# Memory attention and a bilinear feed-forward layer: batch 1's k and v apart, zero products ahead, and a new order of the work

## The chip, the core and the metric

The kernel runs on one core of a Trainium2 chip. The core has a matrix engine (PE, with its weight loads shown apart as PEld), a vector engine (DVE), an engine for activations (ACT), GpSimd (POOL), and SyncE (SP), which here only starts output transfers. All read the on-chip memory SBUF; PE writes to eight accumulator banks called PSUM, from which DVE and ACT read. Transfers from and to HBM are issued by an engine into a queue and run on 16 DMA engines.

The metric is the device time of one execution in microseconds, the median of several runs. Each engine executes its own instructions strictly in the order written; an instruction waits on semaphores for what it needs from other engines or transfers, and what stands behind it on its engine waits too.

## The reference

For each of 8 batches and 8 heads (576 tokens, 64 dimensions a head) the tokens' k and v are pooled into 32 memory slots, then attention runs over the slots, and the joined heads go through a bilinear layer:

```python
a = softmax(phi)                                # over the 32 slots, per token
k_m, v_m = einsum('bhsm,bhsd->bhmd', a, k), ... # the same with v
attn = softmax(q @ k_m.T / 8) @ v_m             # over the slots
x = attn, heads joined: 4608 x 512
out = ((x @ w_a) * (x @ w_b)) @ w_out           # 512 -> 1536 -> 512
```

## The kernel before

**Tiling and stages.** For a batch, `exp_phi` (ACT) makes the exponentials of phi, `exp_sb`. Products of `exp_sb` with k, v and a plane of ones then give, for all heads, the k sums, the v sums and the sums of the exponentials at once (`kv_sums`, tile `pkv`; 72 small products of 64 rows by 32 columns of the array). `take_kv` scales them by the reciprocal of the third part, `kv_transpose` turns them (`pT`, `kvT`). q is turned on DVE (`qT`), `scores` multiplies it with the turned k part (`pscore`), ACT takes the exponential (`E`), and E is normalised over the slots (`A`). The v part is never multiplied with A directly: `fold` multiplies it with the weights `w_a` and `w_b` first (`pva`, cast into `vab0` and `vab1`), so that A times `vab` is at once the input of the bilinear layer. The rows L727 are these products (`pa`, `pb`); ACT casts `pa`, and DVE multiplies it with `pb` into `ht`. From batch 5 on part of the products is made by a scheme of seven instead of eight products (L750). The output product with `w_out` goes the same way (L654), on sums of `ht` (`h_sums`, L638) and of the weights (`w_sums`, L621), two blocks of 128 tokens at a time.

Batch 0 has its own path: `sums` (tile `pk`, L377) and `transpose` (L395), separately for k and v and for two groups of heads. Batch 1 has its q in two parts (320 and 256 tokens), and its scores, exponentials and normalisation are made per part (`scores_half`, L442).

**The order.** `PLAN` (from L18) is a list written out by hand or by a program: each word is one step, and the loop at L785 issues the steps in this order. So the place of a word sets the order on every engine at once. Words used below: `0ks1` is sums of batch 0, group 1, with k (`vs` with v), `0kt1` its turn; `1kv`, `1km0`, `1kvt` are `kv_sums`, `take_kv` and `kv_transpose` of batch 1; `0qt0` a turn of q; `1qh30` a turn of a part of q; `0s0`, `1sh0` scores, `0e0` their exponential, `den` the sums over slots, `nr` the normalisation; `0hv0a` and `1v2b` are folds with w_a or w_b, `hx`, `x` their casts; `a0.1.0`, `b0.1.0` are `pa` and `pb` of batch 0, 128 columns number 1, first part of the tokens; `d3` is three steps of the output product; `h`, `g` are `h_sums` on POOL or DVE; `T`, `V` are `w_sums` on POOL or DVE; `p1`, `k1`, `v1`, `q1.0`, `wa0:256`, `o1` are the loads of phi, k, v, a part of q, of columns 0 to 255 of w_a, of a part of w_out; `F1` is a zero product, `O` makes the block `ones` for the sums over slots, `M` fills the plane of ones of the second k/v buffer.

**Loads.** All input but batch 0's k is loaded by transfers that POOL issues, in one queue, so in order. POOL waits before such an issue until the one eight loads earlier has landed. k and v of even and odd batches lie in two buffers `kv_sb0` and `kv_sb1`, each with its own plane of ones (filled by DVE at L236 and by POOL at L792).

**Zero products.** `fill` (L227) multiplies a zero block `warm` with itself into the PSUM bank that would be taken next, without taking it: 128 by 128 times 128 by 512, result unused. The list before has nine of them, one at the start and eight between 15.9 and 22.6 us. Two calls that follow each other make two tiles on the same bank, and the second waits for the first.

Of the kernel before, what the change touches and what calls it, by code (L numbers as in the profile page):

```python
# [8 lines left out]
F32 = mybir.dt.float32  # L9
F16 = mybir.dt.float16  # L10
# [3 lines left out]
P = 128  # L14
# [9 lines left out]
1qh10 1qh00 o0 o3 1sh0 1eh00 0v1b 1v1b 1x0b1 1eh10 1x0a1 0x1b0 1den00 0x1b1 1x1b1 o4 1den10 o2 a0.6.1 b0.6.0 b0.6.1
b0.5.1 1nr10 1nr00 1x1b0 b0.4.0 a0.7.1 b0.7.1 a0.7.0 a0.5.0 b0.7.0 a1.5.0 b0.5.0 h0.3 b1.5.0 a1.3.0 1qh21 a0.4.1 o5
b1.3.0 1qh31 1qh01 a1.4.0 b0.4.1 a1.1.0 1qh11 a1.2.0 b1.4.0 a1.0.0 b1.1.0 1sh1 0v2a 1eh01 1eh11 0x2a1 b1.0.0 0x2a0
b1.2.0 1den01 a1.6.0 0v2b 0x2b0 0x2b1 b1.6.0 v2 a0.9.1 1v2b 1v2a 1x2b0 1x2b1 a0.11.1 1x2a1 1x2a0 b0.9.1 a0.10.1
a0.9.0 b0.11.1 b0.10.1 b0.9.0 V20 1den11 a1.10.0 b1.10.0 a0.11.0 b0.11.0 a0.8.0 a1.11.0 b0.8.0 b1.11.0 1nr11 d1
1nr01 a0.10.0 d1 V00 a1.8.0 b0.10.0 a1.7.0 d1 b1.8.0 p2 V21 a1.11.1 b1.7.0 b1.11.1 d1 a1.3.1 a1.0.1 a1.2.1 g0.0 d1
b1.3.1 a1.6.1 d1 b1.2.1 b1.0.1 V01 a0.8.1 V10 a1.4.1 a1.9.0 d1 k2 2exp0 2exp1 g0.1 d1 V11 b1.6.1 V31 a1.5.1 p3 g0.2  # L30
b0.8.1 q2 d1 b1.4.1 d3 a1.1.1 b1.9.0 d6 2kv 3exp0 k3 d2 2km0 d1 a1.9.1 2km1 v3 d3 b1.5.1 d1 3exp1 d1 a1.10.1 d2
a1.8.1 2kvt b1.1.1 d2 h1.0 a1.7.1 2qt1 d4 2qt0 2qt3 2v1b 2x1b1 2v0a 2x1b0 T30 2qt2 2x0a1 d12 2x0a0 d4 g2.0 g1.1 2sc
g1.2 2e0 b1.7.1 d1 2e1 g1.3 q3 d2 b1.8.1 d3 b1.10.1 d1 2den0 d1 g2.1 p5 2den1 d1 b1.9.1 d1 2nr0 d5 2v2b 3kv 2v1a
g2.3 2x2b1 3km0 2nr1 2x2b0 2x1a1 d7 3km1 d6 3qt2 2x1a0 2v0b 2v2a 2x0b1 3qt3 d3 3qt0 2x2a1 d3 a2.6.0 d1 b2.6.0 d1
3qt1 a2.4.0 2x2a0 b2.4.0 d1 h2.2 d1 a2.7.0 d2 a2.4.1 d1 2x0b0 b2.4.1 d4 a2.3.0 a2.1.1 3kvt 5exp1 v5 b2.7.0 p4 b2.3.0
a2.8.0 b2.1.1 k5 a2.1.0 d2 a2.2.0 d2 q4 d1 a2.5.0 h3.3 3sc 3e0 d2 b2.2.0 d1 3e1 d2 b2.8.0 5exp0 d1 b2.1.0 v4 d2
a2.10.0 d2 b2.10.0 a2.0.1 a2.11.0 b2.11.0 b2.5.0 3den0 a2.0.0 d1 b2.0.1 h3.0 d1 g3.1 a2.5.1 d1 a2.9.0 k4 b2.5.1 h3.2
b2.0.0 3nr0 a2.11.1 d1 a2.8.1 b2.9.0 d1 3den1 d2 a2.10.1 d2 b2.10.1 d1 3v0a 3nr1 3x0a1 5kv 3x0a0 3v0b 3x0b0 b2.8.1
a2.2.1 d1 q5 d1 4qt0 b2.11.1 4qt3 4exp1 d1 3x0b1 d3 b2.2.1 d1 a2.9.1 d1 4qt1 d2 4qt2 d1 a2.7.1 b2.9.1 g4.3 d1 a2.6.1
h4.0 a2.3.1 d1 g4.1 d1 a3.3.0 d1 h4.2 4exp0 k7 b2.7.1 a3.2.0 d2 b2.6.1 d5 b3.3.0 b3.2.0 d2 4kv p6 3v2a 4km0 d2 3x2a1  # L40
4km1 d11 3x2a0 b2.3.1 d2 4kvt d2 a3.0.0 a3.3.1 v6 5km0 q6 d2 a3.1.0 5km1 k6 h5.0 d5 b3.1.0 a3.1.1 4sc 4e0 b3.0.0 d1
5qt3 d2 b3.1.1 5qt0 d1 a3.0.1 4e1 d3 b3.3.1 d5 3v1b 3v1a 4ed 3v2b 3x1b1 d5 3x1a0 d2 3x1a1 4sm0 d1 5qt1 d2 h5.3 3x2b0
5kvt a3.8.0 4sm1 d1 3x1b0 h5.1 3x2b1 d4 5qt2 d3 a3.6.1 b3.0.1 a3.10.0 d3 a3.4.0 d1 p7 d1 6exp1 d1 b3.8.0 b3.4.0 d1
a3.5.0 b3.6.1 d1 b3.10.0 4tn1 a3.7.0 a3.9.0 h5.2 d1 5sc 4tn0 5e0 d1 b3.5.0 5e1 a3.5.1 a3.11.0 d1 b3.7.0 d3 6qt0 d4
4v0a 4x0a0 4v1b 4v0b 4x0b1 d2 4x1b1 d5 6qt2 d1 4ad d1 5ed d1 a3.4.1 5sm0 b3.5.1 d2 b3.9.0 d1 4x1b0 d3 4x0a1 b3.11.0
d2 q7 d3 6qt1 d1 a3.6.0 a3.2.1 h6.3 6exp0 b3.6.0 d2 b3.4.1 d2 4x0b0 a3.8.1 a3.7.1 d5 a3.11.1 d2 b3.11.1 b3.8.1 d1
5tn0 d2 b3.2.1 4v2b 4v2a 4x2b0 6kv h6.0 4v1a d2 4x2b1 d1 5sm1 4x2a0 6km1 6km0 h6.1 6qt3 d3 b3.7.1 4x1a1 d3 4x1a0
a3.9.1 d2 4x2a1 5tn1 d2 b3.9.1 d3 a3.10.1 a4.0.0 g6.2 a4.2.1 b3.10.1 b4.0.0 d1 a4.3.0 d2 a4.0.1 6kvt b4.2.1 a4.6.0
d5 5ad 5v1a 6sc 5x1a1 h7.3 d1 6e1 d1 5x1a0 d1 7qt0 b4.6.0 d1 6e0 b4.0.1 d6 5T0D d2 h7.0 5v1b 5v0a 5v0b 5x1b0 g7.1
g8.0 g8.3 5x1b1 5T1D g7.2 5x0a0 d3 5x0b0 d6 5x0a1 b4.3.0 d8 5S01D a4.9.1 5T3D v7 a4.7.0 g8.1 b4.7.0 a4.10.1 a4.8.0  # L50
d1 b4.9.1 d1 5x0b1 a4.1.1 d2 5S11D 5S31P b4.8.0 b4.10.1 6ed 5S21P a4.6.1 a4.11.0 d1 b4.6.1 a4.5.0 d1 P5.4.1 7exp0
b4.5.0 b4.11.0 d1 b4.1.1 d3 P5.5.1 P5.4.2 a4.2.0 P5.5.2 d3 5S00P a4.1.0 d1 7qt3 5T2P P5.4.6 a4.9.0 h8.2 d1 a4.4.0
6sm0 d1 P5.5.5 b4.2.0 d1 7exp1 d1 6tn0 d1 b4.9.0 P5.4.5 P5.4.7 d1 P5.5.6 d3 P5.5.3 d1 a4.8.1 d2 b4.1.0 d1 5S10P d1
P5.4.3 P5.4.4 a4.4.1 a4.7.1 5S20P b4.4.1 d2 b4.4.0 d1 b4.8.1 5v2a 7qt2 5v2b 5x2a0 P5.5.7 5x2b0 b4.7.1 d4 5x2a1 6sm1
a4.10.0 a4.3.1 b4.3.1 d2 5x2b1 P5.5.4 P5.1.1 a4.11.1 b4.10.0 h9.3 d1 6tn1 d6 5S30D a4.5.1 d1 P5.2.1 P5.1.6 d1 J5.5
g9.0 a5.10.1 d1 P5.1.5 P5.2.2 d1 b4.11.1 d1 H5.4 h9.1 P5.1.7 d3 P5.1.2 d1 P5.2.5 d2 P5.2.6 d2 P5.1.3 P5.6.1 d1
P5.1.4 d1 P5.2.3 a5.11.0 d1 P5.2.7 d2 P5.7.1 a5.8.0 h9.2 d1 b4.5.1 P5.7.5 P5.6.6 P5.2.4 d3 P5.7.6 d1 P5.6.5 d1
P5.6.2 H5.1 P5.7.3 H5.2 d5 h10.0 P5.7.2 P5.6.7 a5.8.1 P5.3.1 P5.7.7 P5.6.3 b5.11.0 P5.0.1 d3 h10.1 d2 P5.6.4 P5.0.5
P5.3.6 P5.7.4 d1 b5.10.1 P5.0.6 d3 a5.9.0 6ad H5.7 d2 H5.6 P5.0.3 P5.3.2 d1 P5.3.5 d3 P5.0.2 d1 P5.3.7 d2 P5.0.7 d1
h10.3 a5.10.0 d1 P5.3.3 d3 6T0P d1 P5.3.4 d1 P5.0.4 d1 6T1P 6v0a 6x0a0 6x0a1 6T2P 7qt1 7kv 6v2b 6v0b H5.0 7km0 d1  # L60
H5.3 d1 6x2b1 d1 7km1 d4 6x0b0 6x0b1 d1 b5.8.0 6x2b0 d2 6T3P a5.11.1 b5.10.0 7kvt d1 b5.9.0 d3 6S00P d2 6v1a 7sc
6S10D d3 6x1a0 d1 7e1 d1 g11.0 6S30D g10.2 7e0 b5.8.1 6x1a1 d1 b5.11.1 d6 6v2a 7v1a 6v1b 6x2a1 g11.1 d1 6x1b0 6S20D
# [21 lines left out]
def kernel(  # L84
# [196 lines left out]
    def units(b):  # L281
# [269 lines left out]
        def one(f, *a):  # L551
            return lambda: f(*a)
# [289 lines left out]
```

## Time and profile before

| | us |
|---|---|
| median of 3 runs | 235.27 (233.99 to 237.27) |
| span of the profiled execution | 232.1 |
| PE busy | 214.1 (92%) |
| weight loads busy | 163.6 (70%) |
| DVE busy | 195.7 (84%) |
| ACT busy | 169.4 (73%) |
| POOL busy, with its issues of transfers | 138.2 (60%) |

Busy time counts an instruction from its start to its end; PE's products overlap each other, so a busy PE may still not stream at its best. The profile's page also cuts the span into 40 slices and gives the busy share of each in tenths:

```profile
PE   1189879999999998999999999999999999999993
DVE  3543899999987667898988999999999999999942
ACT  2206679987899997589978996977897769785330
POOL 7927233812549597893374099499475991881151
```

A slice is 5.8 us long. PE reads 1 in the first two, where it has little to do, and 9 in nearly all from the seventh on; DVE reads 9 from the seventh to the eleventh; POOL issues the loads in the first two.

### The profile page before, as it was taken

To read this page: it belongs to the slowest core of one execution; us is meant where nothing else is said; L and a number is where in the kernel's file an instruction comes from. 1 tells how busy PE (TensorE), PEld (TensorE's weight loads), DVE (VectorE), ACT (ScalarE), POOL (GpSimd) and SP (SyncE) were. 2 spreads that over 40 slices of the span, in tenths; PEclk is the share of its full clock that TensorE was granted. 3 is DMA by queue.
4 is the path that set the end of the run, shared out by engine and by line. 5 is a ranking of instruction groups with operands and counts; after the bars stand their busy time and mean duration, and the time that the engine had idled before them with its cause. 6 is when DMAs were issued, how large, how long until landed. Compare 5 with 4: busy or idle time off the path is not lost.

```text
span 232.1 us, 7493 instructions
## 1 busy us (share of the span) xinstructions
PE 214.1 (92%) x2906; PEld 163.6 (70%) x2906; DVE 195.7 (84%) x517; ACT 169.4 (73%) x450; POOL 138.2 (60%) x139
## 2 busy tenths in 40 slices
PE   1189879999999998999999999999999999999993
PEld 0143537588778777777777787887778877888882
DVE  3543899999987667898988999999999999999942
ACT  2206679987899997589978996977897769785330
POOL 7927233812549597893374099499475991881151
PEclk9999999999999999999999999999999999999999
DMA  6999999999998999999840902121303303032164
GB/s 229 238 199 256 205 205 205 205 259 258 208 284 138 264 207 243 253 241 254 210 93 4 190 1 65 28 64 32 93 3 90 78 16 92 18 77 55 42 158 111
DMA packets 26259, 34.09 MB, mean 147 GB/s; under 512 B 2000, under 2 KB 20304, under 8 KB 26224
## 3 DMA queue, kind: packets, MB, share of 16 engines
q0 software_dynamic: 19760, 23.14, 53.5%
q1 hardware_dynamic: 5952, 9.70, 16.2%
q10 hardware_dynamic: 512, 0.79, 1.0%
q8 instruction: 22, 0.36, 0.6%
q14 instruction: 13, 0.11, 0.1%
HBM read 42.47 MB, written 9.44 MB: 224 GB/s over the span
## 4 chain that ended last, share of the span: by engine, by line
PE 71%; DMA 17%; POOL 6%; ACT 3%; issue 2%; DVE 1%; POOLq 0%
PE py L654 18%; PE pb L727 11%; PE pa L727 11%; PE pv L654 9%; DMA wb_sb<-in_moe_w_b_dram 6%; DMA kv_sb<-in_k_dram 6%; PE py L750 5%; PE px L654 4%; PE pva L516 4%; DMA kv_sb<-in_v_dram 4%; PE pv L750 3%; POOL h_sums L638 2%; PE pkv L323 2%; PE px L750 1%; ACT vab L548 1%
## 5 line engine op out<-in xcount | busy, mean ns | idle before, releaser
L734 DVE TENSOR_TENSOR ht<-a_sb,pb 128x288 f16<-128x288 f16 (+2 forms) x144 | 60.5, 445 | 9.6 <-PE pb L727 5.3
L727 PEld LDWEIGHTS <-vab 128*128 128x128 f16 x576 | 55.3, 98 | 14.9 <-issue 2.4
L731 ACT CAST a_sb<-pa 128x288 f16<-128x288 f32 (+2 forms) x144 | 55.1, 417 | 13.6 <-PE pa L727 8.9
L727 PE MATMUL pb<-A,vab 128*128 128x288 f16 (+2 forms) x288 | 54.9, 286 | 0.1
L727 PE MATMUL pa<-A,vab 128*128 128x288 f16 (+2 forms) x288 | 54.3, 286 | 0.5 <-DVE A L478 0.4
L548 ACT CAST vab<-pva 128x512 f16<-128x512 f32 x82 | 45.4, 611 | 6.9 <-PE pva L516 6.8
L654 PEld LDWEIGHTS <-h_sums 128*128 128x128 f16 x432 | 41.4, 98 | 9.9 <-issue 2.4
L638 POOL TENSOR_TENSOR h_sums<-ht 128x768 f16<-128x768 f16 x19 | 31.2, 1645 | 21.4 <-DVE ht L734 21.3
L654 PE MATMUL py<-w_sums,h_sums 128*128 128x256 f16 x216 | 38.1, 273 | 0.0
L654 PEld LDWEIGHTS <-ht 128*128 128x128 f16 x324 | 31.2, 98 | 7.5 <-issue 2.2
L654 PE MATMUL pv<-wo_sb,h_sums 128*128 128x256 f16 x216 | 36.4, 273 | 0.0
L638 POOL TENSOR_TENSOR h_sums<-ht,h_sums 128x768 f16<-128x768 f16 x10 | 16.4, 1640 | 11.6 <-DVE h_sums L638 11.5
L755 ACT COPY z<-py 128x288 f32<-128x288 f32 x48 | 19.2, 415 | 2.3 <-PE py L750 1.8
L781 POOL TENSOR_TENSOR ht<-ah,bh 128x288 f16<-128x288 f16 x19 | 13.7, 737 | 10.1 <-DVE ah L759 7.1
L654 PE MATMUL px<-wo_sb,ht 128*128 128x256 f16 x108 | 18.9, 273 | 0.0
L654 PE MATMUL py<-wo_sb,ht 128*128 128x256 f16 x108 | 18.8, 273 | 0.0
L654 PE MATMUL py<-w_sums,ht 128*128 128x256 f16 x108 | 18.4, 273 | 0.0
L661 ACT ACTIVATE u<-py 128x256 f32<-128x256 f32 x36 | 14.4, 399 | 4.0 <-PE py L654 3.9
L425 ACT ACTIVATE E<-pscore 128x288 f16<-128x288 f32 x28 | 9.8, 431 | 9.5 <-PE pscore L412 9.4
L291 ACT ACTIVATE exp_sb<-phi_sb 128x576 f16<-128x576 f32 x16 | 10.9, 692 | 5.2 <-DMA phi_sb<-in_phi_dram 5.2
L300 DVE STREAM_TRANSPOSE qT<-q_sb 128x288 f32<-128x288 f32 x28 | 12.2, 456 | 2.6 <-DMA q_sb<-in_q_dram 2.6
L750 PE MATMUL py<-asum,vab 128*128 128x288 f16 x48 | 13.5, 286 | 0.0
(106 smaller groups left out, 383.0 us busy)
## 6 DMA issues: line engine op xcount, KB each, us to landing
out_dram<-o_sb SPq DMA_DIRECT2D x68, 128.0 KB, 2.4
phi_sb<-in_phi_dram POOLq DMA_DIRECT2D x8, 576.0 KB, 10.3
kv_sb<-in_v_dram POOLq DMA_DIRECT2D x8, 576.0 KB, 11.2
kv_sb<-in_k_dram POOLq DMA_DIRECT2D x7, 576.0 KB, 13.5
q_sb<-in_q_dram POOLq DMA_DIRECT2D x6, 576.0 KB, 11.9
wo_sb<-in_moe_w_out_dram POOLq DMA_DIRECT2D x6, 256.0 KB, 14.0
wa_sb<-in_moe_w_a_dram POOLq DMA_DIRECT2D x2, 512.0 KB, 14.2
wb_sb<-in_moe_w_b_dram POOLq DMA_DIRECT2D x2, 512.0 KB, 16.6
```

Source lines behind the costliest of these rows:

```text
L291: nc.scalar.activation(out=t["exp"][:, 2 * z:2 * z + 2, :, :], in_=phis[b][:, 2 * z:2 * z + 2, :].rearrange("p c (i m) -> p c i m", m=M), ...
L300: nc.vector.transpose(out=t["qT"][:, hp, :].bitcast(F32), in_=qs[b][:, hp, :].bitcast(F32))
L548: engine_copy(out=vabs[b][z][:, g, lo:hi], in_=pva[:, 0:hi - lo])
L638: engine.tensor_tensor(out=out, in0=in0, in1=in1, op=op)
L654: nc.tensor.matmul(po, lhs[:, i], rhs[:, i], start=first and i == 0, stop=i == KH - 1, skip_group_check=not first)
L661: nc.scalar.mul(out=x, in_=po, mul=scale)
L727: nc.tensor.matmul(ps, vabs[b][x][:, g, P * i:P * (i + 1)], attn[b][:, g, ts], start=(g == 0), stop=(g == 1))
L731: nc.scalar.copy(out=a_sbs[b, i, hf][:, :n], in_=ps)
L734: nc.vector.tensor_tensor(out=ht[:, i, t0:t0 + n], in0=a_sbs.pop((b, i, hf))[:, :n], in1=ps, op=ALU.mult)
L750: nc.tensor.matmul(x[bank][0], lhs, rhs, start=first, stop=True, skip_group_check=True)
L755: nc.scalar.copy(out=x[name], in_=po)
L781: engine.tensor_tensor(out=ht[:, i, t0 + HALF:t0 + S], in0=x["ah"], in1=x["bh"], op=ALU.mult)
```

## The change

The list is new as a whole. Beside it:

- Batch 1's k and v are summed apart: `1kp` sums k with the ones (128 columns), `1vp` sums v alone (64 columns), `1kg`, `1vg` scale them, `1kx`, `1vx` turn them. So the scores of batch 1 can be made ahead of its v. Batches 2 to 7 keep `kv_sums`.
- Both k/v buffers lie in one tile `kv_all` of five planes: k, v of even batches, the ones, k, v of odd batches. One block of ones serves both, so `M` is gone. For odd batches the ones come first in the sums.
- The three blocks `vsum` come from a pool that rotates three buffers instead of two fixed ones.
- 46 zero products instead of nine: 30 ahead of batch 0's first sum, eight from there to the first `pa`, eight behind that.
- The loads go: phi, q, v of batch 0, then `q1.1`, `wa0:256`, `wb0:256`, `wa256:512`, `p1`, `k1`, `q1.0`, `v1`, `wb256:512`, and the other weights. Before, v of batch 0 was followed by the first half weights, `p1`, `k1`, `v1`, then `wa512:1024`, `q1.0`, `wb512:1024`, `wa1024:1536`, `q1.1`, `wb1024:1536`. `O` stands at the front, ahead of `q1.1`.
- Ten operations on sums (of `h`, `w`, `v`, `A`, and products of `ah`, `bh`) go from DVE to POOL.
- `slot_sums` and its branch in `kv_sums`, which the list did not use, are taken out.

```diff
 PLAN = """
-wb0:256 0qt0 wa0:256 0qt3 wb256:512 0qt1 wa256:512 p1 0exp0 0exp1 F1 0ks0 0kt0 0ks1 0vs1 0vt1 0vs0 0vt0 M k1 F1
-0hv0a 0s0 v1 0qt2 O 0kt1 0e0 F1 0s1 0e1 0hx0a0 0hx0a1 F2 0den10 0den01 0den11 0den00 wa512:1024 0hv0b 0hx0b0 0hx0b1
...
+F1 F1 F1 F1 F1 F1 F1 F1 F1 F1 0qt0 F1 F1 F1 O F1 F1 F1 F1 F1 F1 F1 F1 0exp0 q1.1 F1 F1 F1 F1 F1 0qt1 F1 0qt3 0qt2 F1
+0exp1 F1 wa0:256 F1 0ks1 F1 0ks0 F1 0kt1 0s1 F1 F1 0kt0 0e1 0den11 0vs1 0s0 wb0:256 0e0 F1 0vs0 F1 F1 wa256:512 0den10
+0vt1 0vt0 0den01 0nr11 0hv0a 0nr01 1qh01 F1 0hv0b 0hx0a1 0hx0a0 a0.1.1 p1 0den00 F1 k1 q1.0 0hx0b1 v1 1qh11 0hx0b0 F1
+0nr00 0nr10 0hv1a 0hx1a0 a0.0.1 b0.0.1 wb256:512 1exp1 F1 a0.0.0 wb512:1024 1qh21 a0.1.0 b0.1.0 0hx1a1 1exp0 1kp 1kg0
+a0.2.1 F1 1kg1 a0.3.1 wa512:1024 wa1024:1536 1qh31 F1 wb1024:1536 o3 1qh30 F1 1kx b0.0.0 1qh00 1sh1 1eh01 a0.3.0 1qh20
+1eh11 b0.1.1 F1 1qh10 1den01 1nr01 a0.2.0 1den11 1sh0 1eh10 1vp 1vg1 1vg0 o1 1vx 1nr11 1den10 1eh00 0hv1b 0hx1b0
...
-    kv_sbs = [consts.tile([P, 3, NHP, NI * D], F16, name=f"kv_sb{t}") for t in range(2)]
-    kvs = [kv_sbs[b % 2] for b in range(B)]
+    kv_all = consts.tile([P, 5, NHP, NI * D], F16, name="kv_all")
+    kvs = [kv_all[:, 3 * (b % 2):3 * (b % 2) + 2] for b in range(B)]
+    trios = [kv_all[:, 2 * (b % 2):2 * (b % 2) + 3] for b in range(B)]
...
+        def part_sums(x):
+
+            planes = ((slice(0, 3, 2), slice(1, 2)), (slice(0, 2), slice(2, 3)))[b % 2][x]
+            t["part", x] = [banks.take([P, 2 - x, D], F32, "pkv", hold=True) for _ in range(2)]
+            for i in range(NI):
+                for g in range(2):
+                    for j in range(4):
+                        r, hp = head(g, j)
+                        nc.tensor.matmul(
+                            t["part", x][g][0][32 * j:32 * j + 32],
+                            t["exp"][64 * r:64 * r + 64, hp, i, :],
+                            trios[b][64 * r:64 * r + 64, planes, hp, D * i:D * (i + 1)],
...
+        def take_part(x, g):
...
+            if x == 0:
+                one, ks = ((1, 0), (0, 1))[b % 2]
+                nc.vector.reciprocal(out=t["rphi"][:, g:g + 1], in_=pkv[:, one, 0:1])
...
+        def part_transpose(x):
...
+            for y in range(2 - x):
+                nc.tensor.transpose(out=pT[:, y, :], in_=t["rep"][:, 2 * x + y], identity=ident)
+            nc.vector.tensor_copy(out=t["kvT"][:, xs], in_=pT)
...
-                vsums[b, n] = spare.tile([P, 3, 512], F16, name=f"vsum{n}")
+                vsums[b, n] = vpool.tile([P, 3, 512], F16, name="vsum")
...
-        elif x == "M":
-            nc.gpsimd.memset(kv_sbs[1][:, 2], 1.0 / CS)
```

More of the change, by code (lines that the diff above doesn't have):

```diff
@@ L24 @@
[L24 to L38, printed above, removed]
@@ L235 @@
     make_identity(nc, ident)
-    nc.vector.memset(kv_sbs[0][:, 2], 1.0 / CS)
+    nc.vector.memset(kv_all[:, 2], 1.0 / CS)
     for x in halves:
@@ L306, in q_transpose_half @@
             nc.vector.transpose(out=t["qT"][:, hp, ts].bitcast(F32), in_=q_part(b, hf)[:, hp].bitcast(F32))
-        def slot_sums(z):
-            if z == 0:
-                t["es"] = kvs[b][:, 2, 0, 0:2 * NHP * M].bitcast(F32).rearrange("p (c m) -> p c m", m=M)
-            nc.vector.tensor_reduce(out=t["es"][:, 2 * z:2 * z + 2], in_=t["exp"][:, 2 * z:2 * z + 2].rearrange("p c i m -> p c m i"),
-                                    axis=mybir.AxisListType.X, op=ALU.add)
         def kv_sums():
-            given = "es" in t
-            n = (3 - given) * D
-            t["pkv"] = [banks.take([P, 2 * D + (1 if given else D)], F32, "pkv", hold=True) for _ in range(2)]
+            t["pkv"] = [banks.take([P, 3, D], F32, "pkv", hold=True) for _ in range(2)]
             for i in range(NI):
@@ L330, in kv_sums @@
                         )
-            for g in range(2 * given):
-                for j in range(4):
-                    r, hp = head(g, j)
-                    nc.tensor.matmul(
-                        t["pkv"][g][0][32 * j:32 * j + 32, 2 * D:2 * D + 1],
-                        t["es"][64 * r:64 * r + 64, hp],
-                        one_cs[64 * r:64 * r + 64],
-                        start=True,
-                        stop=True,
-                        tile_position=(64 * r, 32 * j),
-                    )
         def take_kv(gs=range(2)):
@@ new lines, in take_part @@
+        def take_part(x, g):
+            if "rep" not in t:
+                t["rep"] = spare.tile([P, 3, P], F16, name="rep")
+                t["rphi"] = small.tile([P, 2], F32, name="rphi")
+            pkv, bank = t["part", x][g]
+            half = slice(D * g, D * (g + 1))
+            if x == 0:
+                one, ks = ((1, 0), (0, 1))[b % 2]
+                nc.vector.reciprocal(out=t["rphi"][:, g:g + 1], in_=pkv[:, one, 0:1])
+                km = pkv[:, ks].rearrange("p (d e) -> p e d", e=2).unsqueeze(2).to_broadcast([P, 2, 2, 32])
+                out = t["rep"][:, 0:2, half].rearrange("p e (z d) -> p e z d", z=2)
+            else:
+                km, out = pkv[:, 0], t["rep"][:, 2, half]
+            nc.vector.tensor_scalar(out=out, in0=km, scalar1=t["rphi"][:, g:g + 1], scalar2=None, op0=ALU.mult)
+            banks.free(bank)
@@ L472, in normalise @@
             if ("R", 0) not in t:
-                both = spare.tile([P, 3, 512], F16, name="vsum1").rearrange("p z n -> p (z n)")
+                both = vpool.tile([P, 3, 512], F16, name="vsum").rearrange("p z n -> p (z n)")
                 for x in range(2):
@@ L555, in units @@
             u[f"exp{z}"] = one(exp_phi, z)
-            u[f"ps{z}"] = one(slot_sums, z)
+            u[f"{'kv'[z]}p"] = one(part_sums, z)
+            u[f"{'kv'[z]}x"] = one(part_transpose, z)
+            for g in range(2):
+                u[f"{'kv'[z]}g{g}"] = one(take_part, z, g)
             u[f"ks{z}"] = one(sums, z, 0)
```

120 lines of the change are left out of this document (69 added, 51 removed).

## The prediction

> **What bounds the kernel now.** The profiled execution spans 232.1 us; the median of the three runs is 235.27 (233.99 to 237.27). I sum against the span and add the difference, 3.2 us, at the end. I read the busy time by stretches first (start:end, length, then busy time and count of PE, weight loads, DVE, ACT, POOL; granted clock, DMA share, GB/s):
>
> ```profile
> 0.00:20.00 20.00, 8.99 (x213) 4.41 (x213) 8.62 (x22) 3.96 (x7) 14.51 (x24) 1.00 1.09 234
> 20.00:28.00 8.00, 7.30 (x131) 4.25 (x130) 5.33 (x16) 6.07 (x17) 3.39 (x5) 1.00 1.22 207
> 28.00:35.00 7.00, 5.33 (x119) 2.41 (x99) 6.59 (x19) 4.87 (x14) 2.11 (x3) 1.00 1.28 205
> 35.00:66.00 31.00, 31.00 (x420) 23.26 (x426) 30.76 (x83) 27.31 (x78) 12.28 (x13) 1.00 1.21 227
> ```
>
> From 35 to 66 PE and DVE are both full; before 28 neither is. Next I read PE's waits, the first three rows from 28 to 66, the last from 66 to 229 (total, times, longest):
>
> ```profile
> PE pT L363 <- DVE rep L355: 0.7, 1, 0.7
> PE pscore L442 <- DVE qT L306: 0.5, 1, 0.5
> PE pva L516 <- DMA wb_sb<-in_moe_w_b_dram: 0.2, 1, 0.2
> PE pkv L323 <- DMA kv_sb<-in_k_dram: 0.6, 1, 0.6
> ```
>
> So from 34 us PE practically never waits. The end is set by when steady work starts, and by PE's and DVE's work after that. Only the front offers a gain. Then I read PE's timeline there (start, length, engine, line), first to 20 us, then from 20.3 on:
>
> ```profile
> 8.59 1.15 PE L377 MATMUL pk<-kv_sb,exp_sb 64*32 64x128 f16 x36 [6.92 <-ACT exp_sb L291]
> ...
> 15.93 0.61 PE L232 MATMUL pw<-warm 128*128 128x512 f16 x1
> ...
> 16.59 0.41 PE L516 MATMUL pva<-wa_sb,vsum 64*32 64x256 f16 x8
> ...
> 17.88 0.61 PE L232 MATMUL pw<-warm 128*128 128x512 f16 x1
> ...
> 18.55 0.68 PE L412 MATMUL pscore<-qT,vsum 32*32 32x288 f16 x16
> ```
>
> ```profile
> 20.34 1.12 PE L465 MATMUL pD<-E,ones 128*128 128x288 f16 x4 [0.15 <-PE pw L232]
> ...
> 21.95 1.04 PE L232 MATMUL pw<-warm 128*128 128x512 f16 x4
> 23.05 0.28 PE L727 MATMUL pa<-A,vab 128*128 128x288 f16 x1
> ```
>
> Three things stand here. The first real sum starts at 8.59, when batch 0's exponentials are there. A product that must wait for a zero product starts about 0.06 us after that one's end: 15.93 + 0.61 to 16.59, 17.88 + 0.61 to 18.55, although what else the two followers need (DVE copies ending 16.28 and 18.29) had been ready some 0.25 us earlier. And a zero product lasts 0.61 us early and 0.38 (the shortest in its tile's rows) at 21.95: four in 1.04 stand 0.22 apart, while the four 288-column products at 20.34 still stand 0.24 apart against 0.122 later. PE runs at half pace until about 21.4, though the granted clock reads 1.00 throughout.
>
> Last, POOL's issues. A load is issued when the load eight earlier has landed, so these rows tell landings:
>
> ```profile
> 21.48 0.74 POOL L177 DMA_DIRECT2D wb_sb<-in_moe_w_b_dram  x1 [0.24 <-DMA phi_sb<-in_phi_dram]
> 24.16 0.70 POOL L181 DMA_DIRECT2D wo_sb<-in_moe_w_out_dram  x1 [1.93 <-DMA kv_sb<-in_k_dram]
> 27.18 0.70 POOL L181 DMA_DIRECT2D wo_sb<-in_moe_w_out_dram  x1 [2.32 <-DMA kv_sb<-in_v_dram]
> ```
>
> One queue in series: k of batch 1 takes 2.7 us, v 3.0; by the trace's landings half a weight chunk takes 1.3, a whole one 2.5, the larger q part 1.7.
>
> **The zero products.** 30 of the 46 stand before the first sum (0ks1). In the built program each is a tile of its own on the same PSUM bank and waits for the one before on PE's own semaphore. By the rows above one costs 0.61 + 0.06 = 0.664 us cold and 0.38 + 0.06 = 0.435 warm, not its 0.22 of streaming. At half pace throughout: 1.06 (PE's first start) + 30 x 0.664 = 21.0 us. If PE warms after 8: 1.06 + 8 x 0.664 + 22 x 0.435 = 15.9. If the waits cost nothing: 1.06 + 8 x 0.427 + 22 x 0.216 = 9.2. The 0.06 was seen three times, so the chain counts. Whether it warms PE: PE warmed at 21.4 after 3.4 us in which its array streamed about two thirds of the time (zero products 1.28 us, sums of E 0.9) and not after the 3.4 before that (about 40%); the cold chain streams 0.427 of 0.664, 64%. So probably yes, after some 5 us. I take 15.9, against 8.59 before.
>
> [...]
>
> **Batch 0 after it.** 8 more zero products stand between 0ks1 and the first pa, most with a wait behind them: 8 x 0.435 = 3.5 us. Along the path: sums, scale and turn (0.45 + 0.45 + 0.4), copy 0.29, scores 0.45, exponentials 0.71 twice, the v sums and turns 0.6, fold 0.25, cast 0.42, each from its row. With the zero products I walk to the first pa at 24.0, against 23.05. That chain took 14.5 us before, slowed by v (13.3) and wa (16.0), which now are there.
>
> **Loads.** The order becomes v, q1.1, wa0, wb0, wa256, phi 1, k 1, q1.0, v 1, then the rest of the weights. From v's 13.3 with the durations above: wa256 18.6, phi 21.1, k 23.8, q1.0 25.5 (31.1 before), v 28.5 (26.9 before), wb256 29.8, wb512 32.4, wa512 34.9 (29.4 before), all weights at 40.0 (40.1). So batch 1's q no longer holds its scores. POOL now waits for the DVE memset of `ones`, behind the first turn of q (q lands at 9.1), before it issues q1.1 near 10.4; the queue holds v until 13.3, so this costs nothing; without that cover it would be up to 5 us. Batch 2's v comes behind POOL's h0.3, about 42 us, and the queue is full to 46: nothing.
>
> **To six.** I measure progress as array time, 0.42 ns a column (a 64x32 tile an eighth). Before, PE had 6 us of it done at 27.9 and 35 at 62.8. The list anew reaches six with 4.2 us of streaming and 8 zero products behind the first pa (6 to 8 us with their waits); DVE has 8.1 us of instruction times there, which at its packing (48.7 us busy for a sum of 57.4, so 0.85) is 6.9. I take 7.3: six at 31.3, 3.4 late.
>
> **From six to 35.** Before: 34.9 us, with the holes of 28 to 34. After: DVE's instruction times sum to 37.6 (41.6 before, part of it now earlier, and two weight sums of 0.55 on POOL), x 0.85 = 32; PE at its pace of 35 to 62.8 (27.4 us for 25) is 31.8. Both give 32, so 2.9 us come back. All weights and batch 1 are there by then.
>
> **Behind 35.** Streaming is the same, 156 us. Splitting batch 1's pkv adds 72 small tiles whose columns are the same; one turn is copied in two parts (+0.15 us of DVE). Ten operations move from DVE to POOL, 4 us less and 9 more; POOL was at 60%. PE had no wait to lose there but 0.8 us (k of batch 5, and small ones); on the other side, the shortest distance between a turn's issue and its use falls from 0.75 to 0.43 us of PE work, below DVE's copy of 0.36 plus the turn itself, at two places. Between -0.8 and +1.5, taken as nothing. The free POOL memset, the shared ones and the three rotating buffers cost nothing: POOL and DVE were idle or not waited for there.
>
> Sum: 31.3 + 32 + (232.1 - 62.8) = 232.6, time 235.8.
>
> **Rivals.**
> 1. *PE stays cold through the chain* (slower). The chain ends at 21.0, the first pa comes near 29.8, six at 37: 238.3, time 241.5. It decides where the array's share that warms PE lies above 64%; bounds from the trace are 40 and 66. Chance 0.17.
> 2. *PE warms and cools again*, since the warm chain streams only 0.216 of 0.435, half the time, and the steps after it less. A mean of 0.55 us for a product ends the chain at 17.6; six at 33: 234.3, time 237.5. No stretch of before with less than half after warming shows either way. Chance 0.2. [...]
> 3. *The waits hide* and the first sum starts near 9.2. Then v's landing at 28.5 decides: six at 29.3, 230.6, time 233.8. With another 3 us found behind 35 it would be faster by 2%. Chance 0.15.
> My forecast has 0.48.
>
> **Numbers.** 2% (4.7 us) is about what a measurement of this kernel can tell from no change: under 230.6 is faster, over 240.0 slower. Faster needs rival 3 with everything at its good end: 0.09. Slower takes most of rival 1 and a little of rival 2: 0.2. The forecast's own range is 234 to 238; with most of rival 3 below it and most of rival 1 above, 232 to 241.
>
> **What would show it.** Zero products 0.43 to 0.67 us apart at the start, the first pk at 15 to 17 (21 for rival 1, under 10 for rival 3); the first pa at 23 to 26; 288-column products in pairs 0.12 apart from then on; no DMA wait of PE from 28 to 35, DVE full from about 25; PE without waits behind 60. A PE stall of over 1 us behind 60, or a first sum at 9 with steady work before 28, would make the prediction wrong.

## The result, and the profile after

| | before | after |
|---|---|---|
| median of 4 runs, us | 234.63 (233.81 to 237.27) | 270.83 (269.89 to 272.71) |
| span of the profiled execution | 232.1 | 268.1 |
| PE busy | 214.1 (92%) | 238.8 (89%) |
| DVE busy | 195.7 (84%), 517 instructions | 212.8 (79%), 504 instructions |
| POOL busy | 138.2 (60%) | 156.2 (58%) |

The changed kernel takes 1.155 times as long (95% interval 1.148 to 1.163). Medians here and below are over all runs of a kernel, ratios over its fast runs alone; of the changed kernels' runs only two of e1's five, the profiled one among them, were slow, over 1.5% above its fastest.

First the page's busy tenths in 40 slices, now 6.7 us each, with the granted clock in tenths:

```profile
PE   7998678899999999799697998889976999599994
DVE  4302256899996676599989999999999999999972
POOL 5583320036584945699365599578874696645251
PEclk9999659999999999999999999999999999999999
```

PE is busy from the first slice on, with zero products, but 9s without a break to the end, as before, do not come. DVE, which read 9 from 29 to 64 us, gets there at about 54 us. The clock is cut in the fifth and sixth slice. The same stretches that the prediction began with (start:end, length, busy time and count of PE, weight loads, DVE, ACT, POOL; clock, DMA share, GB/s):

```profile
0.00:20.00 20.00, 17.29 (x30) 3.07 (x30) 5.33 (x10) 2.54 (x3) 13.02 (x24) 1.00 1.07 231
20.00:28.00 8.00, 6.58 (x193) 3.64 (x193) 1.77 (x7) 1.83 (x5) 2.46 (x4) 1.00 1.25 205
28.00:35.00 7.00, 4.59 (x39) 1.50 (x39) 2.91 (x11) 1.52 (x5) 2.10 (x3) 0.60 1.26 206
35.00:66.00 31.00, 28.49 (x453) 17.13 (x452) 24.19 (x65) 23.32 (x64) 7.86 (x7) 0.93 0.68 123
```

In the first 20 us PE runs 30 instructions, all zero products, where it ran 213. From 35 to 66, full before, DVE has 24.19 us of 31 and the transfers move 123 GB/s against 227. PE's timeline at the front:

```profile
1.06 19.17 PE L232 MATMUL pw<-warm 128*128 128x512 f16 x30 [1.06 <-DVE warm L196]
...
20.29 1.15 PE L403 MATMUL pk<-kv_all,exp_sb 64*32 64x128 f16 x36
...
27.00 0.41 PE L403 MATMUL pk<-kv_all,exp_sb 64*32 64x64 f16 x30
29.30 0.28 PE L403 MATMUL pk<-kv_all,exp_sb 64*32 64x64 f16 x6 [1.89 <-issue]
29.50 1.25 PE L232 MATMUL pw<-warm 128*128 128x512 f16 x2
...
34.27 0.66 PE L756 MATMUL pa<-A,vab 128*128 128x288 f16 x2 [0.94 <-DVE vab L574]
```

The chain of 30 takes 19.2 us, 0.64 each from first to last. The first pa comes at 34.3, 14.0 us after the first sum; before it was 14.5. Behind 82 us, where PE had next to no wait before, PE's waits now are (total, times, longest):

```profile
PE pb L756 <- DVE ht L763: 3.8, 2, 2.3
PE py L683 <- DVE h_sums L667: 2.1, 2, 1.4
PE pkv L315 <- DMA kv_all<-in_k_dram: 1.9, 1, 1.9
PE py L683 <- DVE o_sb L694: 1.9, 1, 1.9
PE py L779 <- DVE al L788: 1.7, 1, 1.7
PE pv L779 <- DVE vsum L559: 1.5, 1, 1.5
```

With three smaller rows it is 16.2 us, 14.3 of it for DVE. And DVE's own groups tell of what. Two forms of sums, first in before, then in after (behind the count: busy us, mean ns of one, idle us before):

```profile
L638 DVE TENSOR_TENSOR h_sums<-ht 128x768 f16<-128x768 f16 x17 | 9.2, 549 | 0.1
L502 DVE TENSOR_TENSOR E<-E,sum 128x512 f16<-128x512 f16 x4 | 2.7, 682 | 0.0
...
L667 DVE TENSOR_TENSOR h_sums<-ht 128x768 f16<-128x768 f16 x18 | 15.5, 874 | 0.2
L528 DVE TENSOR_TENSOR E<-E,sum 128x512 f16<-128x512 f16 x4 | 8.9, 2213 | 0.0
```

The same instruction on the same shape takes 1.6 and 3.2 times as long. Over all DVE sums whose two inputs lie in SBUF this is about 20 us, counted against the shortest of each such row. DVE is busier by 17 us with 13 instructions fewer.

Progress is told by array time (as the prediction defines it: what the real products so far take at 0.42 ns a column, which is 0.122 us for 288 columns, the distance of warm products in before). The table has the us at which PE reaches a mark, with the kernels of the first four experiments:

| | first pk | first pa | 6 us | 35 | 100 | 191 | 35 to 191 |
|---|---|---|---|---|---|---|---|
| before | 8.6 | 23.0 | 27.9 | 62.8 | 133.0 | 227.7 | 164.9 |
| after | 20.3 | 34.3 | 45.7 | 79.6 | 155.9 | 263.7 | 184.1 |
| e1, zero products in one tile | 9.8 | 23.8 | 34.8 | 69.3 | 144.9 | 255.6 | 186.3 |
| e2, none ahead | 9.1 | 22.1 | 31.6 | 69.4 | 145.6 | 255.1 | 185.7 |
| e3, none at all | 9.2 | 19.8 | 29.5 | 64.3 | 139.9 | 250.6 | 186.3 |
| e4, before with 30 ahead | 20.9 | 32.1 | 37.1 | 72.0 | 142.3 | 237.1 | 165.1 |

So after loses 16.8 us up to 35 us of array time and 19.2 behind. Each row is one trace. Kernels whose order agrees up to there (e3, and e5, e15 and e17 below) reach 35 at 64.3 to 66.5 us, so differences of under some 2 us in a stretch tell nothing.

### The profile page after: what moved, and what is told of

Same layout as the page of the kernel before. It is cut to its first block, busy times and chain, and to the rows that moved or that the text cites. A ratio compares the mean times of both kernels' runs of the same rounds, so it can differ in the third digit from the quotient of the medians.

```text
span 268.1 us, 7697 instructions
## 1 busy us (share of the span) xinstructions
PE 238.8 (89%) x3015; PEld 167.6 (62%) x3015; DVE 212.8 (79%) x504; ACT 170.9 (64%) x450; POOL 156.2 (58%) x152
## 5 line engine op out<-in xcount | busy, mean ns | idle before, releaser
L760 ACT CAST a_sb<-pa 128x288 f16<-128x288 f32 (+2 forms) x144 | 56.2, 414 | 25.7 <-PE pa L756 17.7
L756 PE MATMUL pa<-A,vab 128*128 128x288 f16 (+2 forms) x288 | 55.5, 290 | 1.1 <-DVE vab L574 0.9
L574 ACT CAST vab<-pva 128x512 f16<-128x512 f32 x82 | 46.4, 608 | 6.2 <-PE pva L542 5.9
L667 POOL TENSOR_TENSOR h_sums<-ht 128x768 f16<-128x768 f16 x18 | 29.6, 1653 | 34.6 <-DVE ht L763 31.6
L683 PE MATMUL py<-w_sums,h_sums 128*128 128x256 f16 x216 | 34.7, 273 | 2.1 <-DVE h_sums L667 2.1
L683 PE MATMUL pv<-wo_sb,h_sums 128*128 128x256 f16 x216 | 35.2, 273 | 0.0
L232 PE MATMUL pw<-warm 128*128 128x512 f16 x46 | 25.2, 548 | 2.9 <-DVE warm L196 1.1
L810 POOL TENSOR_TENSOR ht<-ah,bh 128x288 f16<-128x288 f16 x21 | 16.0, 769 | 18.1 <-DVE bh L788 11.0
L667 DVE TENSOR_TENSOR h_sums<-ht 128x768 f16<-128x768 f16 x18 | 15.5, 874 | 0.2
L232 PEld LDWEIGHTS <-warm 128*128 128x128 f16 x46 | 4.6, 107 | 17.5 <-issue 15.9
```

Of the source, the lines that this page charges most:

```text
L232: nc.tensor.matmul(pw[:, :cols].rearrange("p (c n) -> p c n", n=P), warm, zeros, start=True, stop=True)
L574: engine_copy(out=vabs[b][z][:, g, lo:hi], in_=pva[:, 0:hi - lo])
L667: engine.tensor_tensor(out=out, in0=in0, in1=in1, op=op)
L683: nc.tensor.matmul(po, lhs[:, i], rhs[:, i], start=first and i == 0, stop=i == KH - 1, skip_group_check=not first)
L756: nc.tensor.matmul(ps, vabs[b][x][:, g, P * i:P * (i + 1)], attn[b][:, g, ts], start=(g == 0), stop=(g == 1))
L760: nc.scalar.copy(out=a_sbs[b, i, hf][:, :n], in_=ps)
```

## The experiments

**The front.** The theory then held was that the chain delays the front and that this pulls the list's timing apart, so that DVE and POOL come to meet; the rival, that the new list makes them meet by itself. e1 keeps all 46 zero products but lets consecutive ones write one tile, so that none waits for the one before:

```diff
         def peek(self, shape, dtype, name):
             n = next(x for x in self.order if x not in self.held)
-            return psum.tile(shape, dtype, name=name, tag=f"bank{n}")
+            if (n, self.uses[n]) not in self.peeked:
+                self.peeked[n, self.uses[n]] = psum.tile(shape, dtype, name=name, tag=f"bank{n}")
+            return self.peeked[n, self.uses[n]]
```

> The changed kernel, with zero products that follow each other on one PSUM bank writing one tile, so that none waits for the one before; the same 46 products in the same places. Theory (the waits between the zero products delay the front, and the delay pulls apart the list's timing, so that DVE's f16 sums meet POOL's later on): the 30 products ahead stand 0.43, later 0.22 us apart, the first sum starts at 9 to 10 instead of 20.3, the first pa before 24, no DVE f16 sum is lengthened by a POOL sum (19.2 us of that in the changed kernel), and the time falls from 270.8 to 226 to 236. Rival (the new list itself makes DVE and POOL meet): the front comes back, some 12 to 18 us, but DVE's f16 sums stay long and the time is 250 to 258.

e2 takes the 30 zero products ahead of `0ks1` out of the list, e3 all 46, and e4 puts 30 of them in front of the list before. The list's first words in e2 and e3, against after, and in e4, against before:

```diff
-F1 F1 F1 F1 F1 F1 F1 F1 F1 F1 0qt0 F1 F1 F1 O F1 F1 F1 F1 F1 F1 F1 F1 0exp0 q1.1 F1
+0qt0 O 0exp0 q1.1
...
-wb0:256 0qt0 wa0:256
+F1 F1 F1 F1 F1 F1 F1 F1 F1 F1 F1 F1 F1 F1 F1 F1 F1 F1 F1 F1 F1 F1 F1 F1 F1 F1 F1 F1 F1 F1 wb0:256 0qt0 wa0:256
```

> The changed kernel without the 30 zero products ahead of batch 0's first sum; the 16 behind it stay as they are, with their waits. Theory: the first sum starts at 8.6; the chain to the first pa runs at half pace for lack of warming, first pa at 20 to 24; time 228 to 240, with at most a few us of lengthened DVE sums. Rival (the list itself): first sum at 8.6, DVE's sums as long as before this edit, time 250 or more.

> The changed kernel without any zero product. Theory: first sum at 8.6, and PE at half pace to about 25 us since little runs there; time 228 to 242. If the clock stays low for longer (the changed kernel's record shows 0.5 to 0.6 granted in two slices near 30 us), it is 5 us or more above the run that keeps the 16. Rival (the list itself): 250 or more.

> The kernel before, with 30 zero products ahead of its list and nothing else. Theory of the chain: they take 1.06 to 20.2 us as in the changed kernel, the first sum starts at 20.3 instead of 8.6. Theory of the pulled-apart timing: loads and POOL's own work run ahead of a late PE, so DVE's f16 sums, none of which met a POOL sum before, meet some, and the time is more than 12 us longer: 247 to 262. Rival (a late front only shifts everything behind it): 235 + 6 to 12 = 241 to 247, no DVE sum lengthened.

Measured: e1 260.48 us (256.81 to 262.05; ratio to before 1.097, 1.090 to 1.105), e2 262.73 (1.120, 1.111 to 1.129), e3 256.29 (1.092, 1.085 to 1.100), e4 244.21 (1.041, 1.033 to 1.049). The rival won in all four (e1 lies 2 us above the range that it gave). In the table, 35 to 191 is 184 to 186 us in the four kernels with the new list, whatever their front, and 165 in the two with the old one, e4's late front included. Up to 35, the zero products cost 15.3 of the 16.8 us (79.6 to e3's 64.3). How this divides is less certain: by the traces 10.3 are their waits for each other (after to e1) and 5.0 the products themselves (e1 to e3), but e1's trace is of its longest run; with 257.99 us, the middle of its three shortest times, the two are 12.8 and 1.7. The rest of the change leaves 1.5 us there, which one trace each cannot tell from nothing. e1's chain also shows what the waits did:

```profile
1.06 8.67 PE L237 MATMUL pw<-warm 128*128 128x512 f16 x30 [1.06 <-DVE warm L196]
9.78 0.68 PE L408 MATMUL pk<-kv_all,exp_sb 64*32 64x128 f16 x36
```

Its products start 0.427 us apart up to the tenth and 0.216 from the eleventh, at 5.2 us, on. So PE warmed here, where products followed without a gap; in after, streaming 0.427 of every 0.64 us, it did not in 19 us.

**DVE and POOL.** In the kernel before, none of the 79 DVE sums with both inputs in SBUF ran while POOL ran a sum; in after 30 of 65 did, and all the long ones are among them (22 are over 15% longer than the shortest of their shape). POOL's sums of 128x512 that met one lasted up to 1.46 us, against 1.15. DVE's two-input operations with one input from PSUM met POOL's sums some 150 times in either kernel and kept their length: in after those of 128x288 with f16 inputs have a mean of 446 ns with a meeting (91 of them) and of 446 without (53). One meeting in e3, by the timelines of DVE, POOL and PE:

```profile
111.04 3.31 DVE L527 TENSOR_TENSOR E<-E,sum 128x512 f16<-128x512 f16 x1
114.45 0.78 DVE L531 STREAM_TRANSPOSE A<-E 128x576 f32<-128x576 f32 x1
...
110.55 3.24 POOL L666 TENSOR_TENSOR h_sums<-ht 128x768 f16<-128x768 f16 x2
...
116.64 0.41 PE L755 MATMUL pb<-A,vab 128*128 128x288 f16 x2 [2.19 <-DVE ht L762]
```

DVE's sum starts 0.5 us into the first of two POOL sums and ends 0.56 us after the second; PE then stands 2.19 us for what DVE has queued behind it. Whether POOL's reading is the cause was tried by e5 (list of e3) and e6 (before), in which POOL's sums (DVE's stay) wait for the same data but read two columns of each block:

```diff
+    def summed(engine, out, in0, in1, op):
+        if engine is nc.vector:
+            engine.tensor_tensor(out=out, in0=in0, in1=in1, op=op)
+            return
...
+        ends = [x[..., ::x.shape[-1] - 1] if len(x.shape) == 2 else x[:, :, ::x.shape[-1] - 1] for x in (in0, in1)]
...
+        nc.gpsimd.tensor_tensor(out=e, in0=ends[0], in1=ends[1], op=op)
+        if n > 400:
+            nc.gpsimd.memset(idle[:, 0:(1274 * n // 1000 - 519) // 2 * 2], 0.01)
+        nc.gpsimd.memset(out, 0.01)
...
-        engine.tensor_tensor(out=out, in0=in0, in1=in1, op=op)
+        summed(engine, out=out, in0=in0, in1=in1, op=op)
```

> The changed kernel without zero products (256.29 us, 19.1 us of lengthened DVE sums), and each POOL sum now reads only two columns of each block and spends the rest of its old time on writing constants, so POOL's busy time and what it waits for stay while its long reads of SBUF go; the sums' values are left out. Theory, that a DVE sum with both inputs in SBUF stands still while a POOL sum reads SBUF, and that this is the cost behind the front: the lengthening falls under 3 us, the stretch from 35 us of array time to the end falls from 186.3 to 165 to 171 us, the time is 236 to 243. Rival, that the new order itself makes PE wait for later results and the long DVE sums are only what one sees of a DVE that is behind: the stretch stays over 180, the time 251 to 258.

> The kernel before with the same edit of POOL's sums (values left out). No DVE sum met a POOL sum there, so by the theory there is nothing to win: 231 to 238 us, the stretch behind 35 us of array time 161 to 167 (164.9 before). Were the short reads a gain by themselves, for instance by results that come earlier, it would be under 229, and the gain of the run beside it would have to be read less that.

Measured: e5 247.94 us (1.058, 1.049 to 1.067), e6 237.15 (1.012, 1.004 to 1.019). DVE's groups in e5 are back at their old means:

```profile
L146 DVE TENSOR_TENSOR h_sums<-ht 128x768 f16<-128x768 f16 x18 | 9.6, 547 | 0.2
L146 DVE TENSOR_TENSOR E<-E,sum 128x512 f16<-128x512 f16 x4 | 2.7, 673 | 0.0
```

30 DVE sums still meet POOL's work there, 20 of them one of its short sums, and none is longer: E's sum has a mean of 673 ns, where e3 has 2190. So in these runs it is POOL's long reads that hold DVE's sums with two inputs in SBUF. But 35 to 191 fell from 186.3 only to 176.5, between the theory's and the rival's numbers; behind 130 us of array time it is as before (64.5 to 63.6 us), between 60 and 130 it is not. POOL's time fell with the edit too (156.2 to 126.9 us busy), which e6 had as well (138.2 to 115.6) and won nothing by. In the old order PE hardly waits, though, so e6 does not exclude that part of the 9.8 us in the new one came from POOL's results being there earlier.

The next four cross order and engines: 40 sums stand on another engine than before, 27 on POOL and 13 on DVE by the words of the lists (e7's expectation has 25 and 15). e7 and e10 give e3's list the old engines, e8 and e9 give the old list the new ones, e9 and e10 with the short reads. Two places of e7's 40 words, which all keep their places:

```diff
-T20 T00 a0.9.1
+V20 V00 a0.9.1
...
-6ed 6sm0 5S11P d6
+6ed 6sm0 5S11D d6
```

> The changed kernel without zero products, its order kept, but each of the 40 sums that stand on another engine than before (25 from DVE to POOL, 15 the other way) back on its old engine. Theory: that no DVE sum meets a POOL sum belongs to order and engines together, so that the old engines in the new order meet as well: lengthening 10 us or more, 248 to 262 us. Rival, that the new division of the sums makes the meetings: lengthening under 5 us, 236 to 244.

> The kernel before, its order kept, with the 40 sums on the engines that the new list gives them. Theory: meetings appear in the old order too, lengthening 6 us or more, 240 to 256 us. Rival, that only the new order makes DVE and POOL meet: lengthening under 2 us, 232 to 238.

> The old order with the new engines (249.09 us, 11.8 us of lengthening), with POOL's sums reading two columns of each block only (values left out). Theory, the new engines cost the old order nothing but the meetings: 235 to 240 us, as the old engines with the same edit (237.15), lengthening under 1 us. Rival, the new engines also bring results later where PE needs them: over 243.

> The new order with the old engines and no zero products (261.2 us, 15.9 us of lengthening), with the same edit of POOL's sums (values left out). Theory, meetings are a good half of what the new list costs and the rest belongs to the new order, in which PE asks for results too early, whichever engine makes the sums: 245 to 252 us, as the new engines with the same edit (247.94). Rival, that the rest comes from the new engines: under 242.

Time from 35 to 191 us of array time (and median time):

| order, engines | sums whole | POOL's reads short |
|---|---|---|
| old, old | 164.9 (234.63) | 165.6 (237.15) |
| old, new | 174.8 (249.09) | 169.2 (240.97) |
| new, old | 187.4 (261.20) | 180.3 (253.46) |
| new, new | 186.3 (256.29) | 176.5 (247.94) |

In each but the first row the reads cost 5.6 to 9.8 us. e7 and e8 came out as the theory had them: old engines meet in the new order, new engines in the old one. That none met belonged to the old order and the old engines together. e9 missed its 235 to 240 by one: moving the sums costs the old order 3.6 us more than the meetings. e10 missed upwards too. With the reads short, the new order costs 14.7 us with the old engines and 10.9 with the new ones (against 165.6).

**The rest of the new order.** 11.6 us stay in e5. Is DVE late there for its load? e13 and e14 were to shorten DVE's sums as well:

```diff
+        ends = [ends_of(x) for x in (in0, in1)]
...
+        if engine is nc.vector:
+            e = ends_of(out)
+            engine.memset(out, 0.01)
+        engine.tensor_tensor(out=e, in0=ends[0], in1=ends[1], op=op)
```

> The new list without zero products, with the sums of both POOL and DVE short: a sum on DVE writes a constant and reads two columns of each block (values left out), so DVE has some 10 to 15 us less to do and everything waits for what it waited for. Theory, DVE is late in the new order for its load: the stretch from 35 us of array time to the end falls from 176.5 us (POOL's sums short alone) to under 170, the time to 238 to 242. Rival, the order asks for results within their latency: the stretch stays at 173 to 177, the time 244 to 248.

> The same edit of the kernel before, as a control (values left out). PE has no waits to lose there behind 35 us of array time: the stretch stays at 163 to 166 us (165.6 with POOL's sums short alone), the time 234 to 238.

They took 267.43 and 267.09 us, and tell something else: a constant of 128x768 took DVE 698 ns against 549 for the sum, so DVE became heavier, in e14 by 25.4 us busy for 29.9 us of time, in e13 by 20.3 for 19.5. In both, a microsecond more on DVE was about a microsecond more at the end. e15 and e16 then lighten DVE, by 36 additions of the output (for pv and px; py keeps its own):

```diff
-            nc.vector.scalar_tensor_tensor(out=o, in0=po, scalar=scale, in1=x, op0=ALU.mult, op1=ALU.add)
+            if x is u5:
+                nc.vector.scalar_tensor_tensor(out=o, in0=po, scalar=scale, in1=x, op0=ALU.mult, op1=ALU.add)
+            else:
+                nc.scalar.mul(out=o, in_=po, mul=scale)
```

> The new list without zero products, POOL's sums short, and 36 of the 54 additions of the output's parts (o_sb from pv and px, 0.41 us each) taken from DVE: ACT scales the product instead and the addition is left out (values left out). DVE has 15 us less to do, ACT some 15 us more, from 171 of 246 us. Theory, DVE is late in the new order for its load: from 35 us of array time to the end under 170 us (176.5 before this edit), the time 237 to 242. Rival, the order asks for results within their latency, whatever DVE's load: 173 to 178 us, the time 244 to 249.

> The same edit of the kernel before with POOL's sums short (values left out), as a control. PE has hardly a wait to lose there: the stretch stays at 163 to 167 us (165.6), the time 234 to 239. If ACT becomes late for its 15 us more, it is over 239, and the run with the new order would have to be read less that.

e15 took 249.00 us, e16 237.32; 35 to 191 is 178.1 and 166.4. DVE's load is not it: with 10 us less on DVE, PE waits at the same places for `h_sums` and `ht`. e17 moves a few words of e5's list at two of them:

```diff
-a3.4.1 d1 4x1b0 d3 b3.0.1 h5.3 d3 a3.9.0 d3 b3.9.0 4x1b1 a3.10.0 b3.10.0 d6
+a3.4.1 b3.0.1 h5.3 d1 4x1b0 d3 a3.9.0 b3.9.0 4x1b1 a3.10.0 b3.10.0 d3 d3 d6
...
-4v2a p6 4x2a1 6qt3 4v1b 4v0a q7 4x0a0 a3.11.1 d4 4tn0
+4v2a 4x2a1 6qt3 4v1b 4v0a 4x0a0 a3.11.1 d4 4tn0 p6 q7
```

> The new list without zero products and with POOL's sums short (247.94 us), with two places of the order mended: the product b3.0.1 and the sum h5.3 that needs it go a few words forward and two output steps a few words back, so that PE has some 1.4 us of other work between them (it waited 2.4 us for h5.3 at 118 us and lost another 1.7 us by the clock of 0.5 that followed); and POOL issues the loads p6 and q7 (1.5 us) behind the normalisation of batch 4's E instead of ahead of it, so that DVE does not wait 1.15 us for it and PE not 0.6 and 1.25 us for DVE. Theory, the rest of the loss is single places where the order asks within the latency: 2 to 5 us less, 243 to 246 us, and the clock stays at 1.0 around 120 us. Rival, such a hole only moves on to the next wait: 247 to 249 us.

245.12 us, and 35 to 191 is 172.9. The two places of the order were worth 3.6 of the 11.6 us by the traces, 2.8 by the medians; PE's wait of 2.4 us for `h_sums` is gone, and so is the clock of 0.50 from 120.3 to 123.7 us that followed it in e5. The other 8 us were not mended one by one; that they are such places too is likely from the waits that remain (5.2 us behind 64 us, all for results of DVE or ACT), not shown.

**Zero products in the old list.** e11 is the kernel before without its nine, e12 with 22 more at the head in one call.

```diff
-wb0:256 0qt0 wa0:256
+F22 wb0:256 0qt0 wa0:256
```

> The kernel before without its nine zero products. The walk of batch 0 stays cold (0.61 us a 512-column product) in both, so the nine, about 5 us of PE's time in places where it waits anyway, are worth nothing either way: 233 to 236.5 us. If they keep the clock up behind the first product of the bilinear layer, their lack costs 2 us or more: over 236.5.

> The kernel before with 22 zero products at the head in one call, so in one tile and with no wait among them. By the run with one tile (0.427 us each up to the tenth, 0.216 us then) they end near 1.1 + 10 x 0.427 + 12 x 0.216 = 8.0 us, ahead of the first sum at 8.6, and PE starts it at full pace: each 36 of its products take 0.68 instead of 1.15 us, three of them on the path, so 0 to 2 us less: 232.5 to 235 us. Rival, the products bring a wait for instructions as in the runs with the new list (1.9 and 3.2 us) or the walk waits for DVE and ACT as before: 234.5 to 238.

e11 234.55 us (ratio 1.001, 0.997 to 1.004), e12 233.78 (0.998, 0.995 to 1.000). Neither differs by what can be told. e12's first 36 sums do run at full pace (0.68 us, 1.15 in before), but batch 0's path waits 2.60 us for DVE's scaling next, the clock is cut (0.50 from 11.2 to 21.5 us), and the first pa comes at 23.3 against 23.0. No version beats the kernel before.

## Why the prediction was wrong

By its own steps, us:

| step | forecast | measured | off by |
|---|---|---|---|
| the zero products end, the first sum starts | 15.9 | 20.3 | +4.4 |
| from there to the first pa | 8.1 | 14.0 | +5.9 |
| first pa to six | 7.3 | 11.4 | +4.1 |
| six to 35 | 32 | 33.9 | +1.9 |
| behind 35 to the end of the span | 169.3 | 188.5 | +19.2 |
| span | 232.6 | 268.1 | +35.5 |

**Behind 35, the step that failed most.** "Between -0.8 and +1.5, taken as nothing." The step counted what changes on each engine (streaming the same, ten operations net from DVE to POOL, "POOL was at 60%") and held an engine with time to spare for free. The count was off: 14 go net (DVE's sums with both inputs in SBUF fall from 79 to 65, POOL's sums rise from 81 to 95), which by the means of before is an estimated 16 us more for POOL, not 9. And it did not ask whether two engines may run such sums side by side. The trace of before could not show the price, since none met; that none of 79 met, with POOL's sums busy 100.6 of 232 us, was itself the sign that the order avoided it. Its bound "no wait to lose" was read from an order whose places fit, and the list was new as a whole. What stood against it: behind 93 us PE reads 9 in every slice but the last, DVE 8 or 9 in all but the last two, so that more work on DVE went to the end (19.5 us for 20.3 in e13, 29.9 for 25.4 in e14). In e3, whose stretch from 35 to 191 is 2.2 us longer than after's and 21.4 longer than before's, 9.8 us went with POOL's reads (e5) and 11.6 stayed. Of these e17 shows some 3 to be two places of the order; the rest belongs to the new order and engines, its places not shown one by one.

**"So probably yes, after some 5 us."** The chain did not warm: rival 1's chain, forecast at 21.0, measured 20.3. The bounds taken from before, 40 and 66%, did not exclude it, and the chain's 64% lay below the upper one. The warming after eight products that the 15.9 is added up from is shown by no run: e1's unbroken chain reached full pace at its eleventh product, 4.2 us after the first, and the chain that waits stayed at half pace for all of its 30, 19 us.

**The walk.** It was shortened from 14.5 to 8.1 because v and wa had landed. e3 took 10.6 for it, at half pace (its first 72 sums kept PE busy for 1.80 us, 72 at half pace in before for 1.90; its trace's clock records begin at 24.0) and with 1.2 us for `wb`. In after two more things came, both in the rows above: 1.89 us in which PE waited for nothing that the profile shows, and half pace behind it. Rival 2 had PE warm and cool again, but within the chain and for 1.7 us; here it came behind the chain and cost more. The next view has it, the stretches of 1 us of after (columns as above, the clock third from the end):

```profile
27.00:28.00 1.00, 0.41 (x30) 0.29 (x30) 0.00 (x0) 0.37 (x2) 0.00 (x0) 1.00 1.36 201
28.00:29.00 1.00, 0.00 (x0) 0.00 (x0) 0.00 (x0) 0.00 (x0) 0.00 (x0) 1.00 1.38 199
29.00:30.00 1.00, 0.70 (x7) 0.25 (x7) 0.28 (x1) 0.00 (x0) 0.64 (x1) 0.67 1.26 208
30.00:31.00 1.00, 0.89 (x3) 0.10 (x1) 0.00 (x0) 0.00 (x0) 0.71 (x2) 0.50 1.25 208
...
39.00:40.00 1.00, 0.79 (x4) 0.23 (x2) 0.10 (x1) 0.92 (x3) 0.19 (x1) 0.71 1.24 205
```

A hole of 1.9 us is followed by 10 us at a clock of 0.50 (29.3 to 39.6). An estimate from these times: if PE could have worked throughout, half pace cost at most 2.5 us up to the first pa and 2.7 of the step to six, and 1.1 more before 22.5 us, where PE was still cold. With the hole that is up to 5.5 of the walk's 5.9 us and 2.7 of the 4.1 to six.

The traces also tell where the hole stands. In after, e1 and e4 such a hole stands in front of PE's 450th recorded instruction (products and weight loads), in after, e1, e2 and e3 in front of its 962nd, and each time PE goes on 1.3 to 1.5 us after a 16 KB transfer in the queue that the page calls `q8 instruction` (27.0 to 28.0 us in after, PE goes on at 29.3). In before that transfer ran from 17.1 to 18.1 us and the 450th instruction started at 21.4, without a hole. That PE stood for its own instructions there is the author's estimate from these times; no run varies this.

**Right:** the loads, from POOL's issues:

```profile
23.82 0.70 POOL L181 DMA_DIRECT2D wo_sb<-in_moe_w_out_dram  x1 [1.91 <-DMA kv_all<-in_k_dram]
25.49 0.71 POOL L181 DMA_DIRECT2D wo_sb<-in_moe_w_out_dram  x1 [0.98 <-DMA q_sb<-in_q_dram]
29.36 0.70 POOL L181 DMA_DIRECT2D wo_sb<-in_moe_w_out_dram  x1 [3.16 <-DMA kv_all<-in_v_dram]
```

k 23.8 (forecast 23.8), q 25.5 (25.5), v 29.4 (28.5). "Batch 2's v comes about 42 us: nothing" was not borne out as cover: the transfers fall to 4 GB/s in the page's ninth slice, and k of a later batch makes PE wait 1.9 us; in e3, whose front is 15 us earlier, such waits behind 64 us come to 0.7. Six to 35 was nearly right. And the prediction named what would make it wrong, a PE stall of over 1 us behind 60: there are nine.

## What to carry to other kernels

Before sums are moved to GpSimd or a tuned order is replaced, look in the trace whether VectorE's sums with both inputs in SBUF ever overlap GpSimd's: here none of 79 did, which belonged to the old order and engines, and idle time on GpSimd was not free (in the other three pairings of order and engines its reads cost 5.6 to 9.8 us). In these runs a chain of filler products warmed the array after 4.2 us where nothing stood between them (e1) and not in 19 us where each waited for the one before (after), and in after, e1 and e12 the clock fell again to 0.50 at a hole of 1.9, 3.2 and 2.6 us; in the old list nine or 31 of them were worth nothing (ratios 1.001 and 0.998). Where two engines are full, price a change of order by the shortest distance between each result and its use, not by sums of busy time.

## What the runs showed of the hardware

- A VectorE sum of 128x512 with both inputs in SBUF (E's) took up to 3.40 us beside GpSimd sums in after, against a mean of 0.68 in before. One of 3.31 us in e3 began 0.5 us into the first of two GpSimd sums in a row and ended 0.56 us after the second.
- In after the granted clock reads 1.00 while a PE that has not warmed yet runs products at half pace (0.58 us each in the chain against 0.38 warm); the trace's clock records begin only at 22.5 us there. In the traces of a PE that has warmed, some holes of 1.9 to 3.2 us are followed by 0.50 for 3.4 to 10.3 us (29.3 to 39.6 in after, 18.8 to 29.1 in e1, 11.2 to 21.5 in e12, 120.3 to 123.7 in e5); others are not (2.3 us at 130 in after, 2.2 at 114 in e3).
- PE stood without a releaser for 1.9 us (after), 3.2 (e1), 3.1 (e2), 1.4 (e3) and 0.9 (e4), always in front of its 450th or 962nd recorded instruction and until 1.3 to 1.5 us after a 16 KB transfer in the queue `q8 instruction`; in before and e12 this does not occur.
- VectorE wrote a constant of 128x768 in 698 ns (e13, e14), longer than it added two tiles of that size (549 in before).
